# Sums of the second layer's output: from additions on VectorE to accumulating DMAs into HBM

## Chip, core and metric

The kernel runs on one core of a Trainium2 chip. The metric is the device time of one execution in microseconds: 625.5 us, the median of three runs (625.45 to 625.58). The profile is of one more execution, which took 625.31 us.

## What is computed

Three stages follow one another on 1536 rows (2 sequences of 768) of 512 numbers, all in float32.

```python
# 1 retention, 8 heads of 64
state = gamma * state + einsum('bhd,bhe->bhde', k[:, :, t], v[:, :, t])
y[:, :, t] = scale * einsum('bhd,bhde->bhe', q[:, :, t], state)
# 2 first gated layer, 512 -> 1536 -> 512
x = (x @ w_a) * (x @ w_b) @ w_out
# 3 norm and second gated layer, 512 -> 1536 -> 512
xn = x / sqrt(mean(x * x) + 1e-6) * rms_g
g = xn @ w_gate
out = silu(g) * (xn @ w_val) @ w_out
```

## The kernel before

**Arithmetic.** Float32 operands are split into a rounded part and its remainder (names ending in h and l, as xh and xl), and a product of two matrices becomes three matmuls: high by high, high by low, low by high. The weights come as raw 64-bit words and are turned into float32 by ScalarE and VectorE steps (to_float, line 152); these conversions run all through the kernel, beside the matmuls.

**Tiling.** The rows form three blocks j = 0, 1, 2 of 512 (TB). The hidden width of 1536 forms 12 tiles of 128 (f). Up products, for j = 0 and 1 together through seven products P1 to P7 (slot, line 395) and for j = 2 in quarter steps a1, a2, b1, b2 (unit, line 366), give the hidden tile h of each f. Two tiles f make a group g (G = 2, six groups). When h of both is there, jobs (line 504) queues down jobs (ffn, g, j, m): four parts m for each j, twelve per group, 72 per layer.

**A down job** (down, line 453) runs six matmuls into one of three PSUM banks Y0 to Y2 taken in turn: y is the share of group g in a tile of 128 rows by 512 outputs. Then collect (line 473) takes y out of PSUM. In the first group (g = 0) y is copied into an accumulator acc in SBUF: in the second layer always by ScalarE (ONACT). In the later groups VectorE adds y to acc. After the last group of the second layer, each tile of acc is written to out by a DMA on the SP queue. The very last job is done in two halves, whose second half leaves through the ScalarE queue. In the second layer one tile of acc is always the same 128 rows of out, so out is written once, at the end. The accumulators of the second layer reuse SBUF of the first layer's (HOME), and until() holds their first use back until those are no longer needed.

**Order of the work.** Each engine runs its instructions in the order in which the program writes them (manual schedule). The order around the up products is written out by hand: in EVEN (even f) a down job D follows nearly every product, ODD has none; BEFORE and LAST (line 51) take their place for the last two f of the first layer. SECOND (line 62) is the order of the six units with which the second layer begins; then the twelve down jobs of g = 0 run in a row (do_down in the main loop, lines 769 on), and at the end of the kernel the twelve of g = 5. Between the products a planner (tick and pull, lines 278 to 300) puts conversion steps of the weights into the streams of ScalarE and VectorE: a step is written when the planner's own clock for its engine is less than LEAD ahead of TensorE's, and its inputs are ready within HOLD; EARLY shifts the due times. norm(j) (line 511) runs beside the last down jobs of the first layer: it squares the finished sums (sq), sums them with small matmuls (ms), spreads the scale with others (rb), scales acc and splits it into xh and xl; APART (line 558) is the number of steps between its two large subtractions xl.

**Queues.** SP issues all weight loads (load_w, line 141, three buffers raw, written directly behind the VectorE step that frees a buffer) and the output stores. GpSimd does only a few products of the retention and issues no DMA.

Of the kernel before, what the change touches and what calls it, by code (L numbers as in the profile page):

```python
# [7 lines left out]
F32 = mybir.dt.float32  # L8
# [4 lines left out]
ALU = mybir.AluOpType  # L13
PSUM = bass.MemoryType.PSUM

B, H, S, D = 2, 8, 768, 64
P = 128
NT = B * S
DM = H * D
DFF = 1536  # L20
C = 128
# [8 lines left out]
TPB = TB // P  # L30
# [3 lines left out]
PARTS = KD, TPB  # L34

HOP = 120
LEAD = {"vec": 2600, "act": 1750, "gps": 4000}

LINE = 128
SIGN = -(1 << 31)  # L40
# [7 lines left out]
EVEN = "P1 D P2 D P6 D P7 D P5 D a1 D P3 D a2 D P4 D D b1 D b2 D"  # L48
ODD = "P1 P2 P6 P7 P5 a1 P3 a2 P4 b1 b2"
BEFORE = "P1 D D P2 D P6 D P7 D P5 D D D P3 D P4 D D D"  # L50
LAST = "P1 P2 P6 P7 P5 A1 P3 A2 P4 B1 B2 D D D D a1 a2 D D b1 b2 D D"
PAIR = 1, 0
OUTS = 3
HOME = (2, 0, 1), (2, 1, 0)
EARLY = {"first": 0.4, "even": 1.5, "odd": -0.4, "plain": 1.0, "out": -0.2, "second": 0.8, "t": -0.2}
MORE = 1000
ONACT = 0, 1
APART = 1
HOLD = {"vec": 1500, "act": 1200, "gps": 4000}
URGENT = NF + 0.5  # L60
RS = 5
SECOND = ((1, 1), (0, 1), (0, 0), (0, 2), (1, 2), (1, 0))
WAIT = {1: (3, 1), 0: (3, 3), 2: (6, 2)}
QD, SD = 2, 3

# [2 lines left out]
def retention_glu_swiglu(ctx: ExitStack, tc: tile.TileContext, qk, kv, dq, mask, dg, eye, w1, w2, rg, out):  # L68
    nc = tc.nc
# [21 lines left out]
    vec, act, gps = Engine(nc.vector, "vec", 70, 1.04), Engine(nc.scalar, "act", 100, 0.83), Engine(nc.gpsimd, "gps", 120, 2.2)  # L91
# [6 lines left out]
    def add(o, a, b, engine=vec):  # L98
        engine.tensor_tensor(o, a, b, op=ALU.add)
# [19 lines left out]
    def held(tag, shape, dtype, name):  # L119
        return late.get(tag, one).tile(shape, dtype, tag=tag, name=name)  # L120
# [95 lines left out]
    def conv_up(f):  # L216
        while converting or f % NF != G and f - 1 not in complete:
            yield "wait"
        converting.add(f)
        wt = late["wt"].tile([P, 8, KH], F32, tag="wt", name=f"wt{f}")  # L220
        yield from to_float([(f, 0, lambda: wt[:, 1:6:4, :]), (f, 1, lambda: wt[:, 0:7:6, :])])
        plain = f % NF < G
        if not plain:
            yield "vec"
            add(wt[:, 2], wt[:, 0], wt[:, 6])
            sub(wt[:, 3:5], wt[:, 1:3], wt[:, 0:2])
            yield "vec"
            sub(wt[:, 7], wt[:, 5], wt[:, 4])
            yield "act"
        while may_up[0] < f:  # L230
            yield "wait"
        uh, ul = ups[f] = tuple(one.tile([P, 8, KH], F32R, tag=f"{w}{f % 2}", name=f"{w}{f}") for w in ("uh", "ul"))
        for blocks in (slice(1, 6, 4), slice(0, 7, 6)) if plain else (slice(1, 2), slice(5, 6), slice(3, 5), slice(2, 3), slice(6, 8), slice(0, 1)):
            act.copy(uh[:, blocks], wt[:, blocks])
            yield "vec"
            sub(ul[:, blocks], wt[:, blocks], uh[:, blocks].bitcast(F32))
            w_ready.update((f, o) for o in range(8)[blocks])
            yield "act"
        converting.remove(f)
        complete.add(f)  # L240
# [20 lines left out]
    def task(due, g):  # L261
        tasks.append(Task(due, g))
        tasks.sort(key=lambda t: t.due)

    def until(ok):
        if ok():
            return
        while not ok():
            if not any(t.step() for t in list(tasks)):
                n = [next(g, "done") for g in list(eager)]  # L270
                assert set(n) - {"wait"}
        work["pe"] = max(work["pe"], work["vec"], work["act"])
# [5 lines left out]
    def pull():  # L278
        for t in list(tasks):
            if eager and t.due > URGENT:  # L280
                break
            if max(work[t.on], t.ready) < work["pe"] + LEAD[t.on] + MORE * bool(eager) and t.ready < work["pe"] + HOLD[t.on] and t.step():
                return True
        return False

    def tick():

        for s in list(soon):
            s[0] -= 1
            if s[0] <= 0:  # L290
                soon.remove(s)
                s[1]()
        for g in list(eager):
            got = None
            while got is None:
                got = next(g, "done")
            if got == "done":
                eager.remove(g)
        while pull():
            pass  # L300
# [16 lines left out]
    def prep_t(ffn, y0, y1):  # L317

        b11, b21, b12, b22 = y0[:, 0:2], y0[:, 2:4], y1[:, 0:2], y1[:, 2:4]
        while ffn and not {(1, 0), (1, 1)} <= prepped:  # L320
            yield "wait"
        sub(b11, b12, b11)
        yield "vec"
        sub(b12, b22, b12)
        yield "vec"
        sub(b22, b22, b11)
        yield "vec"
        sub(b21, b21, b22)
        yield "act"
        while not late:  # L330
            yield "wait"
        ts[ffn] = tuple(late["t"].tile([P, 3, 2, TB], F32R, tag=w, name=f"{w}{ffn}") for w in ("th", "tl"))
        for o, b in ((2, b22), (3, b12), (4, b11), (6, b21)):
            while o == 6 and ffn not in plain_done:
                yield "wait"
            hi, lo = right(ffn, o)
            act.copy(hi, b)
            yield "vec"
            sub(lo, b, hi.bitcast(F32))
            x_ready.add((ffn, o))  # L340
            yield "act"
# [24 lines left out]
    def unit(ffn, f, j, banks, vec_rest=False):  # L366
# [3 lines left out]
        n = ffn * NF + f  # L370
        gate_last = n == NF and j == SECOND[0][1]
        rows = ((1, 5), (0, 6)) if ffn == 0 or gate_last else ((0, 6), (1, 5))
# [78 lines left out]
    acc, ys, n_y, collected, todo = {}, {}, [0], set(), []  # L451

    def down(job):
# [16 lines left out]
        collect(job, y, cuts=2 if g == NG - 1 and ffn and not todo else 1)  # L470
        tick()

    def collect(job, y, cuts):
        ffn, g, j, m = job
        if (ffn, j) not in acc:
            until(lambda: j == 0 or (0, 6) in x_ready if ffn == 0 else (1, 2) in prepped if j == 1 else (1, 6) in x_ready)
            acc[ffn, j] = held(f"acc{HOME[ffn][j]}", [P, *((TPB, DM) if ffn else (KD, TB))], F32, f"acc{ffn}_{j}")
        t = acc[ffn, j][:, m]
        chunk, seq = divmod(j * TPB + m, B)
        row = seq * S + chunk * C  # L480
        n = DM if ffn else TB
        for x in range(cuts):
            c = slice(x * n // cuts, (x + 1) * n // cuts)
            if g:
                add(t[:, c], y[:, c], t[:, c])
            elif m % 2 or ONACT[ffn]:
                act.copy(t[:, c], y[:, c])
            else:
                vec.tensor_copy(t[:, c], y[:, c])
            if ffn and g == NG - 1:  # L490
                (nc.scalar if x else nc.sync).dma_start(out[row:row + P, c], t[:, c])
        collected.add(job)
# [18 lines left out]
    def norm(j):  # L511
# [43 lines left out]
        for e in range(0, KD, 2):  # L555
            sub(lo[:, e:e + 2], y[:, e:e + 2], hi[:, e:e + 2].bitcast(F32))
            if e == 0:
                for _ in range(APART):
                    yield "tick"
        prepped.add((1, j))  # L560

    with tc.manual_schedule():

        xf = {}
        with ExitStack() as att:
            ac = att.enter_context(tc.tile_pool(name="ac", bufs=1))
            ap = att.enter_context(tc.tile_pool(name="ap", bufs=3))
            a2 = att.enter_context(tc.tile_pool(name="a2", bufs=2))
# [154 lines left out]
            def sums(n):  # L723
# [3 lines left out]
                else:  # L727
                    task(G - EARLY["t"], prep_t(0, xf[0], xf[1]))

# [16 lines left out]
        for g in range(2 * NG):  # L746
            for f in range(g * G, g * G + G):
                if f % NF >= G or f == NF:
                    task(f - EARLY["first" if f % NF == G else "odd" if f % G else "even"], conv_up(f))
                else:  # L750
                    for s in range(2):
                        if (f, s) not in kinds[:n_conv[0]]:
                            task(f - EARLY["plain"], conv_plain(f, s))
            for f in range(g * G, g * G + G):
                if (f, 2) not in kinds[:n_conv[0]]:
                    task(g * G + G - EARLY["second" if g == NG else "out"], conv_plain(f, 2))
        work.update(dict.fromkeys(work, work["pe"]))

        def whole(ffn, f, j, banks):
            for _ in unit(ffn, f, j, banks):  # L760
                pass
            jobs(ffn, f, j)
# [6 lines left out]
        for ffn in range(2):  # L769
            if ffn:  # L770
                task(NF + G - EARLY["t"], prep_t(1, acc[0, 0], acc[0, 1]))
                for i, (f, j) in enumerate(SECOND):
                    whole(ffn, f, j, ("A0", "A1") if i % 2 else ("B0", "B1"))
                    if j == 2:
                        may_up[0] = NF + f + 2
                    if not any(later == 1 for _, later in SECOND[i + 1:]):
                        plain_done.add(1)
                do_down(len(todo))
            for f in range(G, NF):
# [6 lines left out]
                if ffn == 0 and f >= NF - G:  # L786
                    order = LAST if f % G else BEFORE
                for o in order.split():
# [68 lines left out]
```

## Time and profile before

| | before |
|---|---|
| median of 3 runs | 625.5 us |
| profiled execution, its own time | 625.31 us |
| its span, first to last instruction | 623.5 us |
| TensorE busy | 614.6 us (99%) |
| VectorE busy | 505.1 us (81%) |
| ScalarE busy | 313.7 us (50%) |
| GpSimd busy | 13.1 us (2%) |
| bytes moved by DMA | 54.91 MB |
| read from HBM, written to it | 51.22 MB, 3.15 MB |

PE is TensorE's matmul stream, PEld its weight loads, DVE is VectorE, ACT ScalarE, POOL GpSimd, SP SyncE. A name like acc<-y,acc gives the tile written and those read. L87, L96 and L491 are lines of the kernel; most operations pass through a helper and share its line, so that tiles tell them apart. An idle time in brackets at the end of a row names the engine that was waited for. Matmuls overlap, so one lasts 0.39 us while six take 1.36 us.

### The profile page before, as it was taken

Reading aid. Unit: us, or ns where it says so; the run is one execution under the profiler, and the core shown is the slowest. Engines: PE = TensorE matmul, PEld = TensorE weight load, DVE = VectorE, ACT = ScalarE, POOL = GpSimd, SP = SyncE. Lnnn points to the kernel's source line nnn. Section 1 sums busy time; section 2 is a strip of 40 time slices with the busy share of each in tenths; the row PEclk is TensorE's granted clock in tenths of the full one; section 3 lists DMA queues with packets and bytes.
Section 4 is the critical chain, followed back from the end, with each engine's and each line's share of the span. In section 5 each row is a group of like instructions: output and inputs, shape, how many; then the busy total and the mean of one; then the engine's idle time right before and its main releaser. Section 6 shows DMA issues by size and latency. Waiting matters only on the chain.

```text
span 623.5 us, 8550 instructions
## 1 busy us (share of the span) xinstructions
PE 614.6 (99%) x3260; PEld 505.9 (81%) x3260; DVE 505.1 (81%) x882; ACT 313.7 (50%) x600; POOL 13.1 (2%) x15
## 2 busy tenths in 40 slices
PE   8999999999999999999999999999999999999997
PEld 7788888888888888888877887888888888888886
DVE  4889786998889888799688998698888988787554
ACT  3665554645544642645354668673473464463230
POOL 1330000000000000000000000000000000000000
PEclk9999999999999999999999999999999999999999
DMA  8984112331323113214200032122221331120004
GB/s 343 373 324 135 35 34 68 106 98 34 102 69 101 50 52 102 65 40 132 68 1 1 8 102 95 46 90 67 74 73 58 101 91 58 55 68 1 1 18 185
DMA packets 16456, 54.91 MB, mean 88 GB/s; under 512 B 2080, under 2 KB 2464, under 8 KB 16416
## 3 DMA queue, kind: packets, MB, share of 16 engines
q1 hardware_dynamic: 16128, 54.21, 26.4%
q8 instruction: 25, 0.41, 0.3%
q10 hardware_dynamic: 288, 0.17, 0.1%
q14 instruction: 15, 0.12, 0.1%
HBM read 51.22 MB, written 3.15 MB: 87 GB/s over the span
## 4 chain that ended last, share of the span: by engine, by line
PE 89%; DVE 5%; ACT 3%; DMA 2%; issue 1%; SPq 0%; DVEq 0%; ACTq 0%
PE b L96 29%; PE y L96 28%; PE c L96 27%; PE ya L96 2%; DMA k<-in_kv 1%; DVE acc L87 1%; PE sc L96 1%; DVE u L87 1%; DMA q<-in_qk 1%; PE st L96 1%; DVE xl L87 1%; ACT sq L87 1%; ACT uh L87 0%; DVE sq L87 0%; PE rb L96 0%
## 5 line engine op out<-in xcount | busy, mean ns | idle before, releaser
L87 DVE TENSOR_TENSOR acc<-y,acc 128x512 f32<-128x512 f32 (+1 forms) x121 | 82.3, 682 | 26.6 <-PE y L96 25.6
L96 PE MATMUL c<-xh,uh 128*128 128x512 f32 x256 | 100.5, 393 | 0.2 <-ACT xh L87 0.2
L96 PE MATMUL c<-xh,ul 128*128 128x512 f32 x256 | 99.7, 389 | 0.0
L96 PE MATMUL c<-xl,uh 128*128 128x512 f32 x256 | 98.7, 389 | 0.0
L87 DVE TENSOR_TENSOR ul<-wt,uh 128x512 fp32r<-128x512 f32 (+1 forms) x122 | 60.9, 511 | 18.2 <-ACT uh L87 17.7
L96 PE MATMUL b<-xh,uh 128*128 128x512 f32 x160 | 62.4, 390 | 0.1
L96 PE MATMUL b<-xl,uh 128*128 128x512 f32 x160 | 62.3, 389 | 0.0
L96 PE MATMUL b<-xh,ul 128*128 128x512 f32 x160 | 62.2, 389 | 0.0
L96 PE MATMUL y<-hh,oh 128*128 128x512 f32 x144 | 56.5, 392 | 1.1 <-DVE acc L87 1.1
L96 PEld LDWEIGHTS c<-xh,uh 128*128 128x128 f32 x256 | 48.1, 188 | 10.5 <-ACT xh L87 0.4
L96 PE MATMUL y<-oh,hh 128*128 128x512 f32 x144 | 56.3, 391 | 0.3 <-ACT acc L87 0.3
L96 PE MATMUL y<-hl,oh 128*128 128x512 f32 x144 | 56.2, 390 | 0.1
L96 PEld LDWEIGHTS c<-xh,ul 128*128 128x128 f32 x256 | 48.0, 188 | 10.0
L96 PE MATMUL y<-ol,hh 128*128 128x512 f32 x144 | 56.1, 390 | 0.0
L96 PE MATMUL y<-hh,ol 128*128 128x512 f32 x144 | 56.0, 389 | 0.0
L96 PE MATMUL y<-oh,hl 128*128 128x512 f32 x144 | 56.0, 389 | 0.0
L96 PEld LDWEIGHTS c<-xl,uh 128*128 128x128 f32 x256 | 48.1, 188 | 9.7
L87 ACT CAST uh<-wt 128x512 fp32r<-128x512 f32 (+1 forms) x122 | 53.3, 477 | 0.8 <-DVE wt L87 0.8
L87 DVE TENSOR_TENSOR t<-t,b 128x512 f32<-128x512 f32 x60 | 41.0, 683 | 14.9 <-ACT t L87 8.5
L87 ACT COPY t<-b 128x512 f32<-128x512 f32 x40 | 23.5, 588 | 57.7 <-PE b L96 57.4
L87 ACT ACTIVATE v<-raw 128x512 int32<-128x512 uint32 x72 | 48.0, 666 | 0.0
L96 PE MATMUL b<-th,uh 128*128 128x512 f32 x120 | 46.9, 391 | 0.0
(98 smaller groups left out, 1102.7 us busy)
## 6 DMA issues: line engine op xcount, KB each, us to landing
raw<-in_w SPq DMA_DIRECT2D x72, 512.0 KB, 3.5
q<-in_qk SPq DMA_DIRECT2D x12, 512.0 KB, 6.5
k<-in_kv SPq DMA_DIRECT2D x12, 512.0 KB, 7.4
out<-acc SPq DMA_DIRECT2D x11, 256.0 KB, 2.0
mask_sb<-in_mask SPq DMA_DIRECT2D x1, 512.0 KB, 5.8
dq_sb<-in_dq SPq DMA_DIRECT2D x1, 256.0 KB, 6.8
out<-acc SPq DMA_DIRECT2D x1, 128.0 KB, 1.7
out<-acc ACTq DMA_DIRECT2D x1, 128.0 KB, 1.8
```

Source lines behind the costliest of these rows:

```text
L87: return getattr(self.engine, op)(out, *a, **k)
L96: nc.tensor.matmul(out, *a, **k)
```

## The change

In the second layer collect hands every job to a new function pour. ScalarE copies y out of PSUM into one of four slots of a buffer z (in the SBUF of one of the old accumulators). For g = 0 the slot is stored to its rows of out by a DMA on the SP queue; for g = 1 to 5 a DMA issued by GpSimd adds the slot to these rows in HBM (accum_op add). The second layer has no accumulators in SBUF any more, the last job is no longer cut in two, and the until() ahead of the accumulators falls away for this layer. Besides, some constants of the planner and of the written order are different.

```diff
-LEAD = {"vec": 2600, "act": 1750, "gps": 4000}
+LEAD = {"vec": 2600, "act": 2200, "gps": 4000}
...
-LAST = "P1 P2 P6 P7 P5 A1 P3 A2 P4 B1 B2 D D D D a1 a2 D D b1 b2 D D"
+LAST = "P1 P2 P6 P7 P5 A1 P3 A2 P4 B1 B2 D D D a1 D a2 D D b1 b2 D D"
...
-EARLY = {"first": 0.4, "even": 1.5, "odd": -0.4, "plain": 1.0, "out": -0.2, "second": 0.8, "t": -0.2}
+EARLY = {"first": 0.4, "even": 1.4, "odd": -0.4, "plain": 1.0, "out": -0.2, "second": 0.8, "t": -0.2}
...
-APART = 1
-HOLD = {"vec": 1500, "act": 1200, "gps": 4000}
+APART = 2
+HOLD = {"vec": 1200, "act": 2000, "gps": 4000}
...
-SECOND = ((1, 1), (0, 1), (0, 0), (0, 2), (1, 2), (1, 0))
+SECOND = ((1, 1), (0, 1), (0, 0), (0, 2), (1, 0), (1, 2))
...
+    def pour(job, y):
+
+        _, g, j, m = job
+        if not zs:
+            zs.append(held(f"acc{HOME[0][2]}", [P, 4, DM], F32, "zs"))
+        z = zs[0][:, n_y[0] % 4]
+        chunk, seq = divmod(j * TPB + m, B)
+        row = seq * S + chunk * C
+        act.copy(z, y)
+        if g:
+            nc.gpsimd.dma_start(out[row:row + P], z, accum_op=ALU.add)
+        else:
+            nc.sync.dma_start(out[row:row + P], z)
+        collected.add(job)
+
+    zs = []
+
     def collect(job, y, cuts):
         ffn, g, j, m = job
+        if ffn:
+            return pour(job, y)
```

## Rows read from the trace of the kernel before

**Rows 1.** The profile's page: span, busy time of each engine.

```profile
span 623.5 us, 8550 instructions
...
PE 614.6 (99%) x3260; PEld 505.9 (81%) x3260; DVE 505.1 (81%) x882; ACT 313.7 (50%) x600; POOL 13.1 (2%) x15
```

**Rows 2.** Windows: stretch, us, busy PE, PEld, DVE, ACT, POOL, clock, DMA, GB/s.

```profile
0.00:50.00 50.00, 46.76 (x605) 38.88 (x609) 36.24 (x65) 28.21 (x71) 13.10 (x15) 1.00 0.89 344
...
300.00:350.00 50.00, 48.25 (x230) 38.72 (x230) 38.28 (x73) 25.85 (x39) 0.00 (x0) 1.00 0.04 11
350.00:400.00 50.00, 49.71 (x219) 40.59 (x218) 42.07 (x66) 33.68 (x61) 0.00 (x0) 1.00 0.21 65
...
388.00:604.00 216.00, 216.00 (x953) 178.37 (x952) 171.48 (x304) 108.91 (x205) 0.00 (x0) 1.00 0.19 58
...
603.50:620.00 16.50, 16.38 (x73) 13.23 (x71) 9.57 (x15) 0.74 (x2) 0.00 (x0) 1.00 0.41 159
```

**Rows 3.** The chain of waits, its end: start, us, engine, tile, line.

```profile
603.56 16.33 PE y L96 x72
```

**Rows 4.** Groups: additions on DVE after 390 us; copies into acc on ACT.

```profile
L87 DVE TENSOR_TENSOR acc<-y,acc 128x512 f32<-128x512 f32 x59 | 40.6, 688 | 17.3 <-PE y L96 16.6
...
L87 ACT COPY acc<-y x18: 573/589/610, 73.4 to 388.3; 128x512 f32<-128x512 f32 x18
```

**Rows 5.** The chain of waits, 419 to 447 us.

```profile
419.56 1.56 PE y L96 x6
...
438.85 1.36 PE y L96 x6
440.20 1.36 PE b L96 x6
441.56 2.72 PE y L96 x12
```

**Rows 6.** The timeline of PE, 381 us.

```profile
380.98 0.50 PE L96 MATMUL y<-oh,hh 128*128 128x512 f32 x1 [0.29 <-ACT acc L87]
```

**Rows 7.** DMA issues (KB each, us to landing); the output stores' own.

```profile
raw<-in_w SPq DMA_DIRECT2D x72, 512.0 KB, 3.5
...
out<-acc SPq DMA_DIRECT2D x11, 256.0 KB, 2.0
...
L491 SPq DMA_DIRECT2D out<-acc x12: 332/333/348, 605.7 to 620.4; - x12
...
DMA to landing us min/median/max: 1.7/2.0/2.3
```

**Rows 8.** Waits of the SP queue: us in total, times, longest.

```profile
SPq L146 <- DVE wt L87: 285.4, 41, 16.4
```

**Rows 9.** The timelines of PE and DVE, 320 to 332 us.

```profile
320.55 1.10 PE L96 MATMUL rb<-ident,scale 128*128 128x128 f32 x8 [0.35 <-DVE scale L87]
331.40 0.50 PE L96 MATMUL y<-hh,oh 128*128 128x512 f32 x1 [1.07 <-DVE acc L87]
...
328.93 1.22 DVE L87 TENSOR_TENSOR xl<-acc,xh 128x1024 fp32r<-128x1024 f32 x1
330.06 0.69 DVE L87 TENSOR_TENSOR ul<-u,uh 128x512 fp32r<-128x512 f32 x1
```

**Rows 10.** The timeline's end, and the landing of the last store.

```profile
619.50 0.39 PE L96 MATMUL y<-oh,hl 128*128 128x512 f32 x1
619.92 0.76 DVE L87 TENSOR_TENSOR acc<-y,acc 128x256 f32<-128x256 f32 x2 [0.67 <-PE y L96]
620.71 0.35 ACTq L491 DMA_DIRECT2D out<-acc  x1
...
out<-acc ACTq DMA_DIRECT2D x1, 128.0 KB, 1.8
```

**Rows 11.** Groups of POOL: one of its products, one of its memsets.

```profile
L87 POOL TENSOR_TENSOR vd<-k,dg_sb 128x512 f32<-128x512 f32 x3 | 3.1, 1044 | 11.2 <-DMA k<-in_kv 11.2
...
L847 POOL MEMSET const-float32-1.0<- 128x1 f32 x1 | 0.1, 99 | 0.0
```

More of the change, by code (lines that the diff above doesn't have):

```diff
@@ L54 @@
 HOME = (2, 0, 1), (2, 1, 0)
-EARLY = {"first": 0.4, "even": 1.5, "odd": -0.4, "plain": 1.0, "out": -0.2, "second": 0.8, "t": -0.2}
+EARLY = {"first": 0.4, "even": 1.4, "odd": -0.4, "plain": 1.0, "out": -0.2, "second": 0.8, "t": -0.2}
 MORE = 1000
-ONACT = 0, 1
-APART = 1
-HOLD = {"vec": 1500, "act": 1200, "gps": 4000}
+ONACT = (0, 1)
+APART = 2
+HOLD = {"vec": 1200, "act": 2000, "gps": 4000}
 URGENT = NF + 0.5
 RS = 5
-SECOND = ((1, 1), (0, 1), (0, 0), (0, 2), (1, 2), (1, 0))
+SECOND = ((1, 1), (0, 1), (0, 0), (0, 2), (1, 0), (1, 2))
 WAIT = {1: (3, 1), 0: (3, 3), 2: (6, 2)}
```

## The prediction

> **What bounds the kernel now.** I read busy time first, then the windows, then the chain, and only then single waits. TensorE (PE) is busy 614.6 of 623.5 us, VectorE (DVE) 505.1, ScalarE (ACT) 313.7, GpSimd (POOL) 13.1 [rows 1]. So PE sets the time and everything that leaves it untouched is worth nothing; at most 8.9 us of its idle time can be won. The windows say where that is [rows 2]: 3.24 us in the first 50 us, where the DMA engines are 89% busy with input; 1.75 us between 300 and 350 and 0.29 us between 350 and 400, where the first layer goes over into the second; and the end. From 388 to 604 us, nearly the whole second layer, PE is busy 216.00 of 216.00 us. There the reader is to see the main point of this case: DVE has 171.48 us of work in that stretch and ACT 108.91, and neither costs anything. The granted clock is 1.00 throughout, the upper level (2.4 GHz), so the clock holds no reserve. The chain of waits ends with 16.33 us of y products (72 matmuls, the last group's twelve jobs of six, 1.36 us each), [rows 3], then the last addition on DVE and the way out [rows 10].
>
> My sum stands on the profiled execution: 625.31 us, of which 623.5 are the span and 1.8 lie around it. The median of the runs shown is 625.5, so 0.2 is added at the end.
>
> **The work that moves.** In the second layer 60 jobs add y into the accumulator. An addition takes 688 ns on DVE; a copy of the same size out of PSUM takes 589 ns on ACT [rows 4]. DVE loses 60 x 0.688 = 41.3 us, ACT gains 60 x 0.589 = 35.3 us (the twelve jobs of the group g = 0 are copied by ACT already). All but the last group's twelve, 48, lie between 388 and 604: DVE goes there from 171.5 to 171.5 - 48 x 0.688 = 138 us, ACT from 108.9 to 108.9 + 48 x 0.589 = 137, both 64% of 216. No wait of PE is removed, because PE has none there. Gain: 0. It could cost something: ACT also makes the copies of b that must be done before PE adds to that bank again, and now a copy of y can stand in front of one of them. With 0.59 us against the 1.36 us of one product, and a whole y job between two b products [rows 5], the slack covers it. I take 0, with 0 to +1.5 us (the 0.29 us that PE has lost to ACT once [rows 6], five times over, once per group) for the range.
>
> **The buffers z.** Four slots; the copy of job k+4 waits until the transfer of job k has landed, and behind that copy stands everything else on ACT, and behind ACT stands PE. Around 440 us a y job comes every 2.72 us, with one pair at 1.36 us [rows 5]; the fourth job after another is thus at least 9.5 us later. A slot is busy for 0.59 us plus the transfer, so a transfer may take 8.8 us before PE notices. Hidden.
>
> **Group g = 0.** Twelve jobs in a row, 1.36 us each, now leave through SP as plain stores. A store of 256 KB takes 2.0 us from its issue to landing, an issue keeps SP 0.33 us [rows 7]. Four slots last 4 x 1.36 = 5.44 us; copy, issue and store need 0.59 + 2.0 = 2.6. The difference, 2.8 us, is what SP may wait with a store at its head. SP is in order and carries the weight loads, each behind the DVE step that empties its buffer; such waits are long (285.4 us over 41 of them, up to 16.4) [rows 8], and a store written after such a load stands behind it. But the load is written right behind that DVE step, and the step is planned at most 2.6 us ahead of PE (LEAD for vec), so what a store meets should be about 2.6 us, just inside the 2.8, with two more free PSUM banks behind it. I take 0, with +2 us as the upper end; this is the wait to look for if PE stalls near 375 to 390.
>
> **The transition.** The only long wait of PE, 1.07 us at 331.40, is for DVE to empty a y bank; its addition stood behind a 1.22 us and a 0.69 us subtraction [rows 9]. APART = 2 moves that second large subtraction (xl) one job later, so that an addition comes before it, and HOLD lets DVE take less early conversion work: the wait should mostly go. LAST swaps the fourth of four y jobs with a1 (one product of the same 1.36 us), which brings the fourth square 1.36 us later and so the scale that rb waits for (0.35 us at 320.55 [rows 9]): no gain, perhaps 0.4 us lost. The accumulators of layer two no longer wait for their old tiles, and the 0.29 us at 381 [rows 6] may go or stay. Together I take -0.7 us; ends -2.0 (all 1.75 + 0.29 gone) and +1.0 (the additions, still on DVE in layer one, pushed deeper into the crowd). The other constants (EARLY, LEAD and HOLD for act, the order in SECOND) shift conversions under a full PE: 0.
>
> **The end.** Here is the price. Before, the last matmul ends at 619.89; two half additions take 0.76, ACT issues the last half at 620.71, it lands 1.8 us later at 622.5 [rows 10], and 1.0 us of closing waits follow to 623.5 [rows 1]. That is 3.6 us behind PE. After: a whole copy on ACT 0.59, about 0.05 to hand over, then an accumulating transfer of 256 KB issued by POOL, of duration L from issue to landing, then the same 1.0 us: 1.64 + L, so the end moves by L - 2.0 (1.64 + L less 3.6). The trace has no transfer issued by POOL and none that adds. Bounds: not below a plain store of the same bytes, L = 2.0 [rows 7]; not above a load of 512 KB and then a store one after the other, 3.5 + 2.0 = 5.5, for the transfer must read z and the old sum, 512 KB, and write 256 KB. The nearest row is the 512 KB load, 3.5 us [rows 7]: the same bytes read. To it I add what POOL's issue may cost more than SP's 0.33 us; POOL's instructions run from 0.10 us (a memset) to 1.04 us and above (products) [rows 11], and I take 1.0, so L = 3.5 + 0.7 = 4.2, and the end moves by +2.2 us (ends 0.0 and +3.5).
>
> The Trainium skill, "DMA: Bandwidth & Descriptors", section "Anatomy of one DMA", fits a transfer issued by GpSimd as 2.0 us plus its bytes at 436 GB/s, that is 2.6 us for 256 KB; the end would then move by +0.6. "Collectives: The Full Stack", section "The bandwidth ceiling", says that an adding transfer needs two source reads on one side and so gets half the rate, which makes it an estimated 3.2 us, and +1.2. No row of this trace shows either.
>
> **The pace of the end.** The last twelve jobs come every 1.36 us. POOL must issue faster than that, and a slot must come free in 4 x 1.36 = 5.44 us, so L may be 4.8 us. With L = 4.2 both hold, the second with 0.6 us to spare. This is where the forecast is thin.
>
> **Sum.** 625.31 + 0 (moved work) + 0 (z, g = 0) - 0.7 (transition) + 2.2 (end) = 626.8; with 0.2 for the median 627.0 us.
>
> **The rivals.**
> (a) The pace breaks: the accumulating transfers can't follow the last twelve jobs. For: L has only 0.6 us of room, and POOL's cost is unknown. Against: the stores of before followed at 1.36 us without trouble [rows 7], the DMA engines are 41% busy there [rows 2]. Place: from 605 us on; it decides from an issue above 1.36 us or L above 4.8. With L = 6.5 a slot cycle is 7.1 us, 1.78 per job, so 8 x 0.42 = 3.4 us of stalls and 2.3 us more at the very end: 632.7. An issue of 1.8 us instead costs 12 x 0.44 = 5.3: 632.3. So about 629 to 633.
> (b) A cheap transfer: L near 2.0 to 3.0, and the transition gives back 1 to 2 us. For: a 256 KB store lands in 2.0 and PE's waits at 331 and 381 are the kind that the new order addresses. Against: the transfer moves three times the bytes, and the crowd on DVE at 320 to 335 is the same work in another order. 625.5 - 2.0 + 0.5 = 624.0 at best, 625.5 in its middle; only the last part is faster than 0.2%.
> (c) It doesn't overlap as meant: each accumulating transfer waits until the one before has landed, as if all rows of the output were one. Then 60 of them need 60 x 4.2 = 252 us from about 421.6 on (the first adding job starts at 419.56 [rows 5], and product and copy take 2), the span ends 1.0 later at 674.6, and with 2.0 around it and for the median the time is 676.6. Against: stores to other rows overlapped in the trace, twelve issues 1.36 us apart that each took 1.7 to 2.3 us to land [rows 7].
>
> **Chances.** This kernel's measurement can tell 0.2% (1.25 us) from no change. The likeliest case, the sum above with a hidden second layer and a longer end: 0.50, its own range 625.6 to 628.2, of which 0.30 lies above 626.75. Rival (a): 0.27, all slower. Rival (b): 0.20, of which 0.06 is below 624.25 and the rest within 0.2%. Rival (c): 0.03. So slower 0.60, same 0.34, faster 0.06. Range 625.0 to 632.0: it leaves out the good half of (b), (c) and the far end of (a).
>
> **What would show it.** Right: 388 to 604 still full on PE, with DVE and ACT near 138 and 137 us; a tail behind PE's last matmul of about 5.8 us instead of 3.6; POOL issues 1.36 us apart in the last group, and no wait of ACT for a transfer. Wrong: PE waits for ACT's copies near 375 to 390 (SP's queue), or in the last 16 us (pace); a wait at 331 that stays; a landing of the accumulating transfer outside 2.0 to 5.5 us. A time below 624 would mean that PE won time in a place where I see none to win.

## The result, and the profile after

The changed kernel takes 632.93 us (median of 4 runs, 632.45 to 633.17), the kernel before 625.48 (4 runs, 625.33 to 625.58): ratio 1.0118, 95% interval 1.0101 to 1.0136. It is slower, as forecast, but by 7.5 us, not by 1.5, and lies 0.9 us above the range. The profiled execution took 632.45 us, with a span of 630.7; against 625.31 and 623.5 before, both grew by 7.1 to 7.2 us.

The page of the changed kernel, its span and busy times, answers to [rows 1].

```profile
span 630.7 us, 8741 instructions
...
PE 615.3 (98%) x3260; PEld 506.9 (80%) x3260; DVE 467.6 (74%) x821; ACT 345.1 (55%) x660; POOL 65.0 (10%) x75
```

PE's busy time is the same within 0.7 us, so 6.5 of the 7.2 us are idle time of PE. DVE lost 37.5 us and ACT gained 31.4, somewhat less than the 41.3 and 35.3 of the forecast. The windows of the changed kernel (stretch, us, then busy PE, PEld, DVE, ACT, POOL, clock, DMA share, GB/s) answer to [rows 2] and say where the idle time is not.

```profile
300.00:350.00 50.00, 48.14 (x231) 38.87 (x230) 38.06 (x72) 25.48 (x39) 0.00 (x0) 1.00 0.03 11
350.00:400.00 50.00, 49.70 (x219) 40.67 (x218) 41.31 (x64) 32.77 (x58) 0.00 (x0) 1.00 0.37 127
...
388.00:604.00 216.00, 215.72 (x952) 178.02 (x950) 146.17 (x261) 135.13 (x256) 41.58 (x48) 1.00 0.62 125
...
610.00:622.00 12.00, 10.25 (x46) 8.15 (x44) 0.00 (x0) 4.58 (x9) 6.91 (x8) 1.00 1.09 169
```

The transition, 300 to 400 us, is as full as before (48.14 and 49.70 against 48.25 and 49.71). The second layer is still full: 215.72 of 216.00, while DVE went from 171.48 to 146.17 and ACT from 108.91 to 135.13. What is left is the end, which the timeline of the changed kernel shows (start, us of duration, engine, line, operation; in brackets the idle time before it and what ended it).

```profile
619.87 0.39 PE L96 MATMUL y<-oh,hl 128*128 128x512 f32 x1
619.99 0.59 ACT L87 COPY zs<-y 128x512 f32<-128x512 f32 x1 [0.72 <-DMA out<-zs]
...
621.58 0.59 ACT L87 COPY zs<-y 128x512 f32<-128x512 f32 x1 [1.01 <-DMA out<-zs]
622.46 0.86 POOL L483 DMA_DIRECT2D out<-zs  x1 [0.73 <-ACT zs L87]
```

Two rows from the groups of the same kernel say how it closes: the landing of the last adding transfer after its issue, and POOL's own DRAIN (instructions; shortest, median and longest ns; first start to last start).

```profile
DMA to landing us min/median/max: 4.9/4.9/4.9
...
L872 POOLq DRAIN  x3: 40/102/7446, 622.4 to 630.4; - x3
```

In the kernel before, where POOL issues no transfer, its longest DRAIN lasted 1.38 us:

```profile
L853 POOLq DRAIN  x3: 34/77/1379, 42.5 to 623.2; - x3
```

Put together in times of the span: PE's last product ends at 620.26 (before 619.89, +0.37). The last copy then waits 1.32 us for its slot, takes 0.59, POOL starts 0.29 later at 622.46, the transfer lands 4.9 later at 627.36, POOL's DRAIN, which began together with that issue at 622.44, ends 7.45 later at 629.89, and the span ends at 630.7. The tail behind PE is 10.4 us instead of 3.6; 6.8 and the 0.37 are the 7.2 us.

### The profile page after: what moved, and what is told of

Same layout as the page of the kernel before. It is cut to its first block, busy times and chain, and to the rows that moved or that the text cites. A ratio compares the mean times of both kernels' runs of the same rounds, so it can differ in the third digit from the quotient of the medians.

```text
span 630.7 us, 8741 instructions
## 1 busy us (share of the span) xinstructions
PE 615.3 (98%) x3260; PEld 506.9 (80%) x3260; DVE 467.6 (74%) x821; ACT 345.1 (55%) x660; POOL 65.0 (10%) x75
## 3 DMA queue, kind: packets, MB, share of 16 engines
q1 hardware_dynamic: 16128, 54.34, 26.1%
q0 software_dynamic: 8640, 15.73, 17.1%
## 4 chain that ended last, share of the span: by engine, by line
PE 74%; DVE 8%; issue 8%; ACT 4%; POOL 3%; DMA 1%; POOLq 0%; SPq 0%; DVEq 0%; ACTq 0%
PE y L96 25%; PE b L96 24%; PE c L96 21%; POOL out L483 3%; PE ya L96 2%; DVE acc L87 1%; PE sc L96 1%; DMA k<-in_kv 1%; DVE u L87 1%; DVE wt L87 1%; DVE xl L87 1%; PE w L96 1%; DVE ul L87 1%; ACT xh L87 1%; PE st L96 1%
## 5 line engine op out<-in xcount | busy, mean ns | idle before, releaser
L483 POOL DMA_DIRECT2D out<-zs x60 | 51.9, 871 | 527.5 <-ACT uh L87 442.4
L87 ACT COPY zs<-y 128x512 f32<-128x512 f32 x72 | 42.1, 587 | 42.6 <-PE y L96 26.7
L96 PEld LDWEIGHTS c<-xh,uh 128*128 128x128 f32 x256 | 48.1, 188 | 10.5 <-ACT xh L87 0.4
L87 ACT CAST uh<-wt 128x512 fp32r<-128x512 f32 (+1 forms) x122 | 54.8, 478 | 2.1 <-DVE wt L87 1.9
L87 DVE TENSOR_TENSOR acc<-y,acc 128x512 f32<-128x512 f32 x60 | 40.8, 685 | 9.8 <-PE y L96 9.8
```

Source lines behind the costliest of these rows:

```text
L87: return getattr(self.engine, op)(out, *a, **k)
L96: nc.tensor.matmul(out, *a, **k)
L483: nc.gpsimd.dma_start(out[row:row + P], z, accum_op=ALU.add)
```

## The experiments

My theory after the result (E): the loss is the end alone, and in it the way out through GpSimd: landing, slots and the closing of its queue. Rivals: the changed constants cost time (C); ACT or the engines set the pace of the last jobs (F); the planner's two waiting points that the accumulators had, and that went with them, matter (U, formed when the second run missed).

**e1: the constants alone, put into the kernel before.** The sums stay on DVE.

```diff
-LEAD = {"vec": 2600, "act": 1750, "gps": 4000}
+LEAD = {"vec": 2600, "act": 2200, "gps": 4000}
...
-APART = 1
-HOLD = {"vec": 1500, "act": 1200, "gps": 4000}
+APART = 2
+HOLD = {"vec": 1200, "act": 2000, "gps": 4000}
```

and the same for LAST, EARLY and SECOND.

> The kernel before with the changed constants alone (LEAD, LAST, EARLY, APART, HOLD, SECOND); the sums stay in SBUF on VectorE. Theory E (all of the loss lies behind 605 us, in the adding transfers): 625.5 to 626.0 us, since in the changed kernel TensorE's last matmul ended only 0.4 us later than before. Rival C (constants or the fuller ScalarE cost time in the middle): 628 us or more if it is the constants.

Measured: 626.60 against 625.44, ratio 1.0018 (1.0009 to 1.0027): a miss, by 0.6 us. The new constants without the moved work cost 1.2 us. The windows of e1, PE alone (columns as above without the other engines), and its wait show where some of it is: the second layer is no longer full, and PE waits 0.5 us for ACT's copy s.

```profile
400.00:450.00 50.00, 49.67 (x219) 1.00 0.28 85
450.00:500.00 50.00, 49.51 (x219) 1.00 0.26 74
```

```profile
PE b L96 <- ACT s L87: 0.5, 1, 0.5
```

**e2: the change without its constants.** All the constants of e1 are put back to their old values; the moved sums stay.

> The changed kernel with all constants put back, so the accumulating transfers alone. Theory E: 632 to 633.5 us, as the changed kernel, with the same end (about 10 us behind TensorE's last matmul). Rival C: 626 to 628 us if the constants were the cost.

Measured: 643.44, ratio 1.0287 (1.0273 to 1.0301). Theory E missed by 10 us and C by 15: with the sums moved, the old constants are 10.5 us worse than the new ones. The window of e2 at 400 us, one of PE alone behind its longest wait (us, busy, clock, DMA share, GB/s), and from the timeline one row of ACT and two of PE:

```profile
400.00:450.00 50.00, 42.38 (x173) 33.24 (x172) 33.94 (x61) 28.00 (x55) 6.06 (x7) 0.93 0.44 95
...
430.00:435.00 5.00, 5.00 (x18) 0.72 0.41 52
```

```profile
427.39 0.62 ACT L87 CAST oh<-u 128x512 fp32r<-128x512 f32 x1 [2.58 <-DVE u L87]
...
419.74 0.50 PE L96 MATMUL b<-xh,uh 128*128 128x512 f32 x1 [1.42 <-ACT uh L87]
...
428.06 0.80 PE L96 MATMUL y<-oh,hh 128*128 128x512 f32 x1 [4.99 <-ACT oh L87]
```

PE is idle for 7.6 us here, the longest piece of it 4.99 us for ACT's conversion oh at 427.39. Behind that wait the granted clock is 0.50, the lower level (1.2 GHz), from 428 to 432 us, and 1.00 again from 434 on: the twelve products from 428.06 to 433.06 start 0.45 us apart on the mean instead of 0.23, which is 2.5 us more. Idle time and clock together make about 10 of the 10.5 us. The conversion oh that PE waited for stood at 418.99 in the kernel before and at 418.78 in the changed one. So it was issued 8 to 9 us late; ACT was busy for only 28 of the 50 us, and just before it sat idle for 2.58 us until DVE had made u, so it was late in the order, not crowded out. That spoke for the planner, and rival U.

**e3: the last group by plain stores of SP.** The sums of the first five groups are left out of those twelve jobs.

```diff
-        if g:
+        if 0 < g < NG - 1:
```

> The changed kernel, but the twelve jobs of the last group are stored plainly by SP in place of being added by GpSimd; this leaves the sums of the first five groups out of the output. 48 adding transfers remain, earlier. Theory E: the end shrinks to copy 0.6 + store 2.0 to 2.4 + closing 1.0, so 626.0 to 626.6 us. Rival C: 631 us or more, since the middle is unchanged.

Measured: 625.97, ratio 1.0008 (0.9999 to 1.0017), within 0.1 us of what theory E had. All else is as in the changed kernel, the other 48 adding transfers among it, and the loss is gone but for 0.5 us, which the interval does not tell from zero. Groups of e3: the last plain stores with their landing, and POOL's DRAIN.

```profile
L485 SPq DMA_DIRECT2D out<-zs x3: 332/332/332, 618.5 to 621.2; - x3
...
DMA to landing us min/median/max: 2.0/2.0/2.0
...
L872 POOLq DRAIN  x3: 40/93/5820, 590.2 to 624.0; - x3
```

The DRAIN of 5.82 us is still there. It begins with POOL's last issue at 590.2 and is over by 596, some 28 us ahead of the end, where it costs nothing.

**e4: the last group by plain transfers of GpSimd.** Without adding; the earlier sums are left out as in e3.

```diff
-            nc.gpsimd.dma_start(out[row:row + P], z, accum_op=ALU.add)
+            if g < NG - 1:
+                nc.gpsimd.dma_start(out[row:row + P], z, accum_op=ALU.add)
+            else:
+                nc.gpsimd.dma_start(out[row:row + P], z)
```

> The changed kernel, with the last group's twelve transfers still issued by GpSimd but as plain stores without the addition (the first five groups' sums are left out of the output). Theory E1 (the addition in the DMA engines is what is slow; the closing wait of 3 us belongs to GpSimd's queue): landing about 3 us, no wait of ScalarE for a slot, closing 3.0: 628.5 to 629.5 us. E2 (a transfer issued by GpSimd is slow, adding or not): 632 to 633 us. E3 (the closing wait too belongs to the addition): 626.5 to 627.5 us.

Measured: 629.29, ratio 1.0061 (1.0047 to 1.0075). The groups of e4 again:

```profile
L486 POOL DMA_DIRECT2D out<-zs x4: 542/542/542, 617.5 to 621.6; - x4
...
DMA to landing us min/median/max: 2.3/2.3/2.3
...
L875 POOLq DRAIN  x3: 40/93/5537, 621.6 to 627.6; - x3
```

The last transfer starts at 621.60 and lands at 623.9; POOL's DRAIN goes on to 627.1, 3.2 us longer, and the span ends at 627.9. So GpSimd's queue alone, without any adding, costs 629.29 - 625.97 = 3.3 us, and most of it (4.0 us from landing to end instead of 1.0) lies in the closing. Adding costs 632.93 - 629.29 = 3.6 us more. The time is the one of theory E1, but with some luck: E1 had a landing of 3 us and a closing of 3.0, and the runs show 2.3 and 4.0.

**e9: adding, but half the bytes.** The last group's transfers take 256 of 512 columns; the other half of the last sums is left out.

```diff
+            c = DM if g < NG - 1 else DM // 2
-            nc.gpsimd.dma_start(out[row:row + P], z, accum_op=ALU.add)
+            nc.gpsimd.dma_start(out[row:row + P, :c], z[:, :c], accum_op=ALU.add)
```

> The changed kernel, with the last group's twelve adding transfers cut to the first 256 of 512 columns (the last group's share of the other half is left out of the output). Same number of transfers and of rows, half the bytes. Theory F with bytes as the price: about 0.8 us of the engines per transfer, no wait for a slot, landing 3.0 to 3.5 us: 629 to 630.5 us. If the price is per row, not per byte: as the changed kernel, 632 to 633 us.

Measured: 629.48, ratio 1.0066 (1.0052 to 1.0079). The landing falls to 3.0 us, and ACT no longer waits for a slot: what adding costs falls with its bytes. It does not halve with them: the time that the packets take is 0.85 x 1.36 = 1.16 us of all 16 engines for each transfer, where the expectation had 0.8 and e5, with whole transfers at the same distance, has 1.08 x 1.36 = 1.47 (its DMA share from 608 to 622 us is 1.08). The window of e9 and its transfers:

```profile
610.00:622.00 12.00, 10.11 (x45) 8.05 (x43) 0.00 (x0) 4.70 (x8) 7.76 (x9) 1.00 0.85 97
```

```profile
L484 POOL DMA_DIRECT2D out<-zs x2: 862/862/862, 619.7 to 621.1; - x2
...
DMA to landing us min/median/max: 2.9/3.0/3.1
```

**e5: eight slots instead of four.** It asks whether the 1.32 us that the last copy waits come from the slots (S) or from a pace that the engines can't follow (F).

```diff
-        z = zs[0][:, n_y[0] % 4]
+        if g == 1 and len(zs) == 1:
+            zs.append(held("acc0", [P, 4, DM], F32, "zs2"))
+        n = n_y[0] % (4 * len(zs))
+        z = zs[n // 4][:, n % 4]
```

> The changed kernel with eight slots z in place of four from the second group on (the other four in the space of another old accumulator). Theory F (the DMA engines themselves need about 1.5 us for an adding transfer against 1.36 us of a job, so the last transfers are late whoever waits): ScalarE's waits for a slot go, TensorE's end is the same, and the last landing moves by at most 0.4 us: 632.3 to 633.1 us. Theory S (the four slots set the pace): the 1.3 us that the last copy waited are won, 631.3 to 631.8 us.

Measured: 631.75, ratio 1.0101 (1.0087 to 1.0115), 1.2 us less than with four; S holds, F falls. The waits of ACT from 600 us on (total us, times, longest), first of the changed kernel and then of e5, with the landings of e5 from 612 to 616 us and of its last three transfers:

```profile
ACT zs L87 <- DMA out<-zs: 6.7, 7, 1.2
```

```profile
ACT zs L87 <- PE y L96: 9.4, 12, 1.4
...
DMA to landing us min/median/max: 5.7/5.7/5.9
...
DMA to landing us min/median/max: 5.4/5.5/5.5
...
L486 POOL DMA_DIRECT2D out<-zs x3: 862/862/865, 618.3 to 621.0; - x3
```

With eight slots ACT waits for PE alone, and the last issue comes at 621.02 instead of 622.46. The landing of the last gets longer (5.4 us for 4.9), so not all of that is won, and the closing stays. The landing does not climb from job to job, though: 4.2 us for the first of the twelve, 5.7 to 5.9 in the middle, 5.4 for the last. So the engines keep up with one adding transfer every 1.36 us, although the packets of one take 1.47 us of all 16; a share above 1 says that the packets' times overlap, and their sum is not a pace.

**e8: the last group read back.** Groups 0 to 4 as in the change; before the last group SP loads the sums from HBM into the accumulators' old place, DVE adds the last products, and SP and ACT store as before.

```diff
+        if g == NG - 2 and m == TPB - 1:
+            fetch(j)
...
-            return pour(job, y)
+            return last(job, y, cuts) if g == NG - 1 else pour(job, y)
```

fetch issues four loads from out; last is the addition and the store of the kernel before.

> The changed kernel for groups 0 to 4; before the last group SP reads the sums back from HBM into SBUF, and in the last group VectorE adds y to them and the tiles are stored as in the kernel before, the last one in two halves. 48 adding transfers remain. Theory E (only transfers at the very end cost): TensorE's end as in the changed kernel, 0.4 to 0.8 us later than before, and the old end of 3.6 us: 625.9 to 626.4 us. Rival C (the fuller ScalarE and the traffic cost in the middle): 628 us or more. If the sums come back late, TensorE waits for VectorE in the last 16 us.

Measured: 625.98, ratio 1.0008 (0.9999 to 1.0017). With the whole computation done, and 48 of the 60 jobs still copied by ACT and added in HBM, the loss is gone as in e3. Its chain ends as that of the kernel before [rows 3, 10]:

```profile
603.91 16.33 PE y L96 x72
620.27 0.42 DVE back L87
```

**e10: e2 with the planner's two waiting points put back.** In the kernel before, the code that made an accumulator also called until(...). Where a named tile is not prepared yet, that call has the planner write preparations until it is, and then moves the planner's clock for PE forward to the latest of PE, DVE and ACT. The change dropped it for the second layer. Here it stands in collect again, with the old constants.

```diff
+            if g == 0 and j not in begun:
+                begun.add(j)
+                until(lambda: (1, 2) in prepped if j == 1 else (1, 6) in x_ready)
             return pour(job, y)
```

> The kernel with the accumulating transfers and all old constants (643.4 us), with the two waiting points of the planner put back that the change dropped together with the accumulators: before the first copy of a block j the planner runs all conversions forward until the splits of x are written. Theory U (the dropped waiting points let the weight conversions of the second layer come late, which cost 7.6 us of TensorE between 400 and 450 us, and the changed constants are there to make up for it): 632.5 to 634 us. Rival (the fuller ScalarE delays the conversions, whatever the planner's waiting points): 641 us or more.

Measured: 632.39, ratio 1.0110 (1.0096 to 1.0124), 11.05 us less than e2, and 0.1 below what theory U had given. The window and the waits of e10 are those of the kernel before [rows 2, 6, 9]:

```profile
388.00:604.00 216.00, 216.00 (x954) 178.60 (x953) 143.82 (x256) 134.65 (x255) 41.72 (x48) 1.00 0.61 125
```

```profile
PE y L96 <- DVE acc L87: 1.1, 1, 1.1
...
PE rb L96 <- DVE scale L87: 0.3, 1, 0.3
...
PE y L96 <- ACT zs L87: 0.3, 1, 0.3
```

**e11: e2 with the new LEAD and HOLD of ACT alone.** LEAD 2200 instead of 1750 and HOLD 2000 instead of 1200 for ACT; all else old, and no waiting points.

> The kernel with the accumulating transfers and the old constants (643.4 us), with two constants of ScalarE's planning alone changed as in the change: LEAD for act 1750 to 2200, HOLD for act 1200 to 2000. Theory U2 (these two are what lets the conversions come early again after the dropped waiting points): 632.5 to 634.5 us. If another constant does it (EARLY, HOLD for vec, SECOND): 638 us or more.

Measured: 632.47, ratio 1.0113 (1.0097 to 1.0129); its window from 400 to 450 us is full again:

```profile
400.00:450.00 50.00, 49.99 (x221) 1.00 0.65 144
```

Either of two things makes up the 10.5 us: the waiting points, or an earlier start of ACT's conversions. The change took the first away and gave the second. In e10 and e11 the stores of group 0 still stand in SP's queue among the weight loads, so the stores by themselves are not what held e2's conversions up.

**e12: e8 with the old constants and the waiting points.** The best version that the runs point to: the middle of the change in the old order, and the old end.

> Old constants, the planner's two waiting points put back, accumulating transfers for groups 1 to 4, and the last group added by VectorE to sums read back from HBM: the best that the experiments point to for accumulating transfers. Theory E (DVE's relief is worth nothing, only the end costs): TensorE's end as before (619.9 to 620.0), the old end of 3.6 us, so 625.4 to 625.8 us, no faster than the kernel before. If the relief of VectorE were worth something in the middle: below 624.5 us.

Measured: 625.59 against 625.30, ratio 1.0004 (0.9995 to 1.0013): no faster. Its window shows why that settles the worth of the moved work:

```profile
388.00:604.00 216.00, 216.00 (x954) 178.60 (x953) 143.79 (x256) 134.65 (x255) 41.69 (x48) 1.00 0.65 139
```

DVE is 28 us lighter than in [rows 2], ACT 26 us heavier, PE full in both, and the time is the same within the interval.

## Why the prediction was right in direction and short in size

**Right: the moved work is worth nothing.** PE stayed full from 388 to 604 but for 0.28 us, and e12 takes 625.59 us with DVE relieved. DVE came to 146 us there, not 138: taking an instruction away freed less than its mean length (e12: 27.7 us for 48, 0.58 each, not 0.688). The slots cost nothing in the middle: landings of up to 7.6 us stand beside the weight loads, under the 8.8 that were allowed (9.5 less 0.59 is 8.9). The plain stores of group 0 behind SP's weight loads made PE wait nowhere near 375 to 390. The price is in the end: e3 and e8 take the adding transfers out of the last twelve jobs alone and are back at 1.0008.

**Failed: "then the same 1.0 us".** This is the largest error: the closing takes 3.3 us, not 1.0. POOL's DRAIN after its last transfer ends 2.5 us after the landing, and 0.8 us more follow. It belongs to every kind of transfer tried that GpSimd issues: e4 shows it without adding (4.0 us from landing to end), e3 and e8 show that it is hidden when POOL's last transfer is early. None of my cases had it, not even as a bound; the trace of before, where POOL issues no transfer, holds no row that it could be read from. I had bounded the transfer from both sides and taken the closing over as a constant, though it was to be the closing of another engine's queue.

**Mis-sized: L.** Forecast 4.2, measured 4.9 for the last and up to 5.5 for those before it; the bounds 2.0 and 5.5 held it. With room it is shorter: 3.8 us is the median of the changed kernel's twelve adding transfers between 560 and 600, which come further apart and have hardly a weight load beside them; beside the loads, from 440 to 560, the median is 4.8 and the longest 7.6, so distance alone does not make the room. In the end the records' packet times add up to 1.09 of what 16 engines have, against 0.85 with half the bytes (e9). The nearest row, a load of the same bytes read, came out 0.3 us short of the roomy case. What the crowd adds is the rest: of the last twelve the first lands in 3.9, all later ones in 4.7 to 5.5.

**Failed with L: "With L = 4.2 both hold".** The issue does hold (0.86 us, below 1.36, and below the 1.0 that I took). The slots do not: copy, hand-over and landing, 0.59 + 0.29 + 5.2 = 6.1 us, are over the 5.44 that four jobs last, and ACT waits seven times, the last one 1.32 us behind PE. That is the condition of rival (a), L above 4.8. Its price was too high, though: PE waits nowhere behind 604 us, since its free banks took up ACT's delay (its end, 620.26, is that of e8, 620.24, where no slot is waited for), and e5 puts the whole matter at 1.2 us, not at the 3.4 of stalls that (a) had. That the time fell into (a)'s bracket of 629 to 633 is luck for the most part: the larger term, the closing, is none that (a) had.

**Small: the hand-over**, 0.29 instead of 0.05.

**Failed: the transition, "-0.7".** The wait at 331 did shrink, from 1.07 to 0.71, and the one for the scale at 320.55 went altogether (rb at 321.19 waits for nothing), so the "perhaps 0.4 us lost" did not come there. But others came. PE's main waits in the timeline of the changed kernel:

```profile
329.89 0.50 PE L96 MATMUL y<-hh,oh 128*128 128x512 f32 x1 [0.71 <-DVE acc L87]
348.30 1.10 PE L96 MATMUL rb<-ident,scale 128*128 128x128 f32 x8 [0.74 <-DVE scale L87]
356.89 0.50 PE L96 MATMUL c<-xl,uh 128*128 128x512 f32 x1 [0.30 <-DVE xl L87]
```

The rb at 348.30 is that of the third block, which waited for nothing in the kernel before. These are its sums of squares ms, its scale and its rb, first in the kernel before, then ms and scale in the changed one:

```profile
344.36 0.95 PE L96 MATMUL ms<-ones,sq 128*128 128x1 f32 x8
348.14 0.16 DVE L87 TENSOR_TENSOR scale<-small,scale 128x4 fp32r<-128x4 f32 x1
348.25 1.10 PE L96 MATMUL rb<-ident,scale 128*128 128x128 f32 x8
```

```profile
343.69 1.02 PE L96 MATMUL ms<-ones,sq 128*128 128x1 f32 x8
348.19 0.16 DVE L87 TENSOR_TENSOR scale<-small,scale 128x4 fp32r<-128x4 f32 x1
```

So PE was indeed 0.67 us ahead at 343.69, about the 0.7 of the forecast (0.47 of it are waits that shrank), and gave that back at 348.30: the scale was no earlier, because ACT's square root for it ran at 346.95 (before at 346.90), directly behind a table load of 1.28 us. Then xl, moved one job later by APART, is late itself by 0.30. The 0.29 us at 381 went, and 0.28 for ol at 420.94 came. I had worked out the waits that go and not what is late next. e1 has the same waits, e10 and e11 with the old LAST and APART have neither the 0.74 nor the 0.30; which of the constants makes which was not tried singly. The old order is no worse: e10 has the old constants, and its PE ends at 620.01, 0.25 us earlier.

**Failed: "The other constants ... : 0".** In the sum it came out nearly so, but as two large terms. Dropping the waiting points costs 11 us under the old constants (e2 against e10), and the larger LEAD and HOLD of ACT make it good (e11). I read the accumulators' until(...) as a wait of 0.29 us at most, because that was the one wait that [rows 6] show; in a planned order it was also the place where the planner was made to issue ahead. In the kernel before the same constants, given alone, cost 1.2 us (e1).

By term, against the forecast: closing +2.3, slot +1.3, PE's end +1.1, L +0.7, hand-over +0.2; that is 5.6 of the 5.7 us between the forecast for the profiled execution, 626.8, and its 632.45.

The estimate of 3.2 us for an adding transfer, worked out from the Trainium skill ("Collectives: The Full Stack", "The bandwidth ceiling", on top of the fit in "DMA: Bandwidth & Descriptors", "Anatomy of one DMA"), is below every landing of 256 KB seen, 3.6 at the least between 560 and 600. The half rate itself agrees roughly, as far as the time of the packets goes: the queue rows of the changed kernel's profile page (queue: packets, MB, share of 16 engines over the span) give 17.1% of 630.7 us over 60 adding transfers, 1.8 us each, against 26.1% over 54.34 MB, 0.79 us per 256 KB, on the queue of the plain transfers.

```profile
q1 hardware_dynamic: 16128, 54.34, 26.1%
q0 software_dynamic: 8640, 15.73, 17.1%
```

**Open.** Why POOL's DRAIN ends 2.0 to 3.2 us after POOL's last landing: the runs show when it comes and what hides it, not what it does. How the 1.2 us of e1 divide over its constants was not tried.

## What to carry to other kernels

If a kernel's last transfer moves to another engine's queue, price the closing of that queue too, not the landing alone: here GpSimd's added 2.3 us, beside 2.9 for the longer landing (4.9 against a plain 2.0); let another queue do the last group. Relief of an engine that the bound never waits for is worth nothing, whatever its busy time says. And where a planner writes the order, a wait that is taken out of the code may have moved the order as well: look for what is issued late, not for the wait.

## What the runs showed of the hardware

- The packets of an adding transfer of 256 KB into HBM take about 1.8 us of all 16 DMA engines, 2.3 times as long as those of 256 KB on the plain queue (mean over the changed kernel). That is no limit of the pace: one every 1.36 us is kept up (e5). It lands 3.8 us after its issue with room (560 to 600 us) and, from the second on, 4.7 to 5.5 at one every 1.3 to 1.8 us in the end. With 128 KB it lands in 3.0 (e9).
- Issued by GpSimd without adding, 256 KB land in 2.3 us (e4), against 2.0 from SP (e3). The issue keeps POOL for 0.54 us, with adding for 0.86.
- POOL's DRAIN, which begins with POOL's last issue, lasted 5.5 to 7.9 us in every run in which POOL issued transfers, plain or adding, and 1.38 in the kernel before.
- In e2 TensorE's granted clock was 0.50 (1.2 GHz) from 428 to 432 us, behind 4.99 us without a product, and 1.00 again from 434 on.
